# Two linear-attention and SwiGLU layers on one core: queries kept in matmul banks, and new order tables for the first layer

## The chip, the cores and the metric

The kernel runs on one core of one Trainium2 chip. The metric is the device time of one execution in microseconds. Five engines run their own queues of instructions and wait for each other by semaphores: PE (matrix products), DVE (elementwise and reductions), ACT (activations and scaled copies), POOL (elementwise) and SP, which here only issues DMAs. PE writes its products into eight banks of 128 x 512 fp32 numbers; all other tiles lie in one on-chip arena.

## What is computed

```python
def _A_ref(x, wqkv, wo):                       # H = 32 heads of 16, S = 2048, D = 512
    q, k, v = ...                              # x @ wqkv, by head
    phi = lambda t: jnp.where(t > 0, t + 1, jnp.exp(t)) + 1e-6
    pq, pk = phi(q), phi(k)
    kv = jnp.einsum("bhsd,bhse->bhde", pk, v)
    z = jnp.einsum("bhsd->bhd", pk)
    num = jnp.einsum("bhqd,bhde->bhqe", pq, kv)
    den = jnp.einsum("bhqd,bhd->bhq", pq, z)[..., None] + 1e-6
    return (num / den) @ wo                    # heads joined again
def _B_ref(x, w1, w3, w2):                     # F = 1792
    return (silu(x @ w1) * (x @ w3)) @ w2
x = x + _A_ref(_layernorm(x), ...)
x = x + _B_ref(_layernorm(x), ...)
x = x + _A_ref(_layernorm(x), ...)             # same weights again
x = x + _B_ref(_layernorm(x), ...)
```

## The kernel before

The 2048 rows are 16 tiles of 128 rows. Every product is made of three fp16 products (high x high, low x high, high x low), so each operand is first split: a high part (an fp16 copy, by ACT or POOL) and a low part (value minus high part, a subtraction with two rows as inputs, by DVE or POOL).

One layer has four stages. The **key stage** normalises a tile, splits and transposes it, projects it, forms phi(k) and adds it into a gram matrix. The **state stage** turns the gram matrix into one 512 x 512 matrix that holds keys, values and the output weights (`m_s`), and starts the first queries. The **query loop** does the rest of the 16 query tiles. The **MLP** works on four chunks of 512 rows with a seven-product scheme for blocks of two by two; its row sums (`mlp_rows`) and its products for group after group follow, and layer 0 also prepares the MLP's weights meanwhile.

In the profile of before, layer 0's key stage is 0 to 112 us, its queries 112 to about 230, its MLP until about 600; layer 1's queries are 714 to about 810.

A query tile t goes through these steps (L numbers are lines of before):

- `query(t)`: PE projects it into a bank `pq` (12 matmuls); ACT writes exp (L848, name `e`) and Relu (L849, name `r`) of the bank into two rows of the arena; SP loads the tile for t + 3.
- `phi_q(t)`: DVE joins them, min(e, 1) + r (L864).
- `weigh_in(t)`: DVE multiplies by the key sums z (L1175) and sums each head into `den` (L1178).
- `weigh_out(t)`: reciprocal (L1191), product with it (L1192, on DVE or POOL by the table `norm`), high part (L411 on ACT or L413 on POOL), low part (L1197 on POOL), and a DMA that transposes both (L1202).
- `attn_out(t)`: PE's 12 matmuls with `m_s` into a bank `po`; `attn_add(t)`: DVE adds it to x (L1212), ACT forms mean and squares (L1216, L1217).

Two pools of four banks exist: "w" (`bank`), which serves `pk`, `pq`, `po` of the attention and `ba`, `bb`, `bc` of the MLP in turn, and "acc" (`acc_bank`), which serves the gram sums, the products `pm`, and the MLP's output sums.

The order in the attention is written out and pinned on all five engines: `STATE` and `KEYS` name the steps, and `LOOP` the steps of one turn of the query loop. In layer 0 that is

```python
LOOP = ("p i v f f q o w f a", ...)   # p phi_q(t+3), i weigh_in(t+3), q query(t+4), o attn_out(t),
                                      # w weigh_out(t+3), a attn_add(t), f fill, v settle
```

Each `f` takes the next entry of `FILLS` and does that many pieces of other work: "1" and "2" are steps of the weight preparation (scales, splits L421 and L423, sums L549 to L555 of the weights' blocks, bounds), "r" a step of the first chunk's MLP rows (L1240 to L1243 sums, L1247 high and L1253 low parts). A weight scale is a reduction over partial maxima on DVE (L357), a small product on PE that spreads it (L360, `pm_w`), and small DVE steps (L362 and on). `ENGINES` gives the engine of each numbered step. In the MLP a planner orders the instructions; `HOOKS` gives how much weight work and how many row steps go behind each group, and how late they are due; `TURN` is the order of a group's products P1 to P7 and the copies (L1311) and sums (L1314) out of their banks.

## Time and profile before

| | us |
|---|---|
| runs | 1210.6, 1213.26, 1214.08 (median 1213.26) |
| profiled execution | 1208.15 |
| its span, first to last instruction | 1206.4 |
| PE busy in it | 1147.9 (95%) |
| DVE, ACT, POOL busy | 857.2, 634.8, 474.3 |
| mean granted PE clock | 0.996 |

Busy time is an average over stages with different limits. PE is idle in few places, and only there can another engine set the time; so the table is to be read with views by stretch and by wait. A name such as `arena` is the one on-chip tile that holds nearly all rows, so lines tell more than names do.

### The profile page before, as it was taken

To read this page: it belongs to the slowest core of one execution; us is meant where nothing else is said; L and a number is where in the kernel's file an instruction comes from. 1 tells how busy PE (TensorE), PEld (TensorE's weight loads), DVE (VectorE), ACT (ScalarE), POOL (GpSimd) and SP (SyncE) were. 2 spreads that over 40 slices of the span, in tenths; PEclk is the share of its full clock that TensorE was granted. 3 is DMA by queue.
4 is the path that set the end of the run, shared out by engine and by line. 5 is a ranking of instruction groups with operands and counts; after the bars stand their busy time and mean duration, and the time that the engine had idled before them with its cause. 6 is when DMAs were issued, how large, how long until landed. Compare 5 with 4: busy or idle time off the path is not lost.

```text
span 1206.4 us, 21781 instructions
## 1 busy us (share of the span) xinstructions
PE 1147.9 (95%) x8852; PEld 863.4 (72%) x8852; DVE 857.2 (71%) x1363; ACT 634.8 (53%) x1066; POOL 474.3 (39%) x520
## 2 busy tenths in 40 slices
PE   5999988889999989999999999989899999999998
PEld 2444533678888878888874454447788888888887
DVE  5787999867788897667775459966766745757443
ACT  5677576846454454433456644576543444444432
POOL 5351689721102113233558823885632122012010
PEclk9999998999999999999999999999999999999999
DMA  8976456669732222211306433564432340211000
GB/s 258 331 213 227 114 146 108 156 205 340 225 118 83 95 78 72 113 62 62 80 6 205 105 110 87 110 153 123 128 75 95 151 157 28 80 63 52 1 36 36
DMA packets 163396, 147.43 MB, mean 122 GB/s; under 512 B 129632, under 2 KB 138976, under 8 KB 158688
## 3 DMA queue, kind: packets, MB, share of 16 engines
q1 hardware_dynamic: 163296, 146.04, 41.3%
q8 instruction: 69, 1.13, 0.4%
q14 instruction: 31, 0.25, 0.1%
HBM read 72.48 MB, written 42.07 MB: 95 GB/s over the span
## 4 chain that ended last, share of the span: by engine, by line
PE 61%; DVE 19%; ACT 7%; POOL 6%; DMA 3%; issue 3%; SPq 0%; POOLq 0%; DVEq 0%; ACTq 0%
PE bb L499 19%; PE po L1358 15%; PE bc L499 10%; PE ba L499 5%; PE pk L499 4%; PE gt L499 4%; PE po L1378 3%; DMA arena<-arena 2%; DVE arena L423 2%; DVE arena L1175 2%; POOL arena L1197 1%; DVE arena L864 1%; DMA arena<-in_B_w_dram 1%; DVE den L1178 1%; ACT arena L421 1%
## 5 line engine op out<-in xcount | busy, mean ns | idle before, releaser
L499 PEld LDWEIGHTS <-arena 128*128 128x128 f16 x6360 | 619.7, 98 | 276.6 <-issue 32.6
L499 PE MATMUL bb<-arena 128*128 128x256 f16 x2688 | 332.6, 273 | 8.2 <-ACT arena L1311 6.5
L1358 PE MATMUL po<-arena 128*128 128x256 f16 x1932 | 236.7, 273 | 10.1 <-ACT arena L1270 8.6
L1358 PEld LDWEIGHTS <-arena 128*128 128x128 f16 x1932 | 188.0, 98 | 35.5 <-ACT arena L1270 10.6
L1311 ACT ACTIVATE arena<-bb 128x512 f32<-128x512 f32 x196 | 115.0, 589 | 164.6 <-PE bb L499 134.4
L1272 DVE TENSOR_TENSOR arena<-arena 128x512 f16<-128x512 f32 (+1 forms) x108 | 124.5, 1154 | 98.9 <-ACT arena L1270 98.6
L499 PE MATMUL bc<-arena 128*128 128x256 f16 x1344 | 165.7, 273 | 5.7 <-DVE arena L1212 3.7
L1270 ACT ACTIVATE arena<-arena 128x512 f16<-128x512 f32 x112 | 99.6, 890 | 91.1 <-DVE arena L1285 38.1
L1427 POOL TENSOR_TENSOR arena<-arena 128x512 f32<-128x512 f32 x29 | 44.3, 1528 | 255.3 <-DVE arena L1407 233.7
L1266 ACT ACTIVATE arena<-arena,scalars 128x512 f32<-128x512 f32 x112 | 74.7, 667 | 103.1 <-DVE arena L1314 102.7
L1267 DVE SCALAR_TENSOR_TENSOR arena<-arena,scalars 128x512 f32<-128x512 f32 x112 | 84.8, 757 | 50.6 <-ACT arena L1266 50.3
L1314 DVE TENSOR_TENSOR arena<-arena,bc 128x512 f32<-128x512 f32 x112 | 76.4, 682 | 51.7 <-ACT arena L1311 45.2
L1407 DVE SCALAR_TENSOR_TENSOR arena<-po,scalars,arena 128x256 f32<-128x256 f32 (+1 forms) x170 | 91.6, 585 | 13.4 <-PE po L1358 10.9
L499 PE MATMUL po<-arena 128*128 128x512 f16 x384 | 89.8, 384 | 6.3 <-DMA arena<-arena 4.7
L499 PE MATMUL pk<-arena 128*128 128x512 f16 x384 | 90.0, 386 | 3.2 <-DMA arena<-arena 1.9
L499 PE MATMUL pq<-arena 128*128 128x512 f16 x384 | 89.1, 384 | 0.7 <-DMA arena<-xt_d 0.7
L499 PE MATMUL gt<-arena 128*128 128x512 f16 x384 | 87.8, 379 | 1.6 <-ACT arena L920 1.0
L499 PE MATMUL ba<-arena 128*128 128x256 f16 x672 | 86.4, 273 | 0.0
L476 ACT ACTIVATE arena<-arena,nb_all,rs_all 128x512 f32<-128x512 f32 x64 | 50.4, 807 | 33.7 <-POOL nb_all L473 30.7
L423 DVE SCALAR_TENSOR_TENSOR arena<-arena,scalars 128x512 f16<-128x512 f32 (+2 forms) x60 | 53.2, 901 | 20.5 <-ACT arena L421 20.4
L1253 POOL TENSOR_TENSOR arena<-arena 128x512 f16<-128x512 f32 (+2 forms) x30 | 46.5, 1574 | 36.6 <-DMA arena<-arena 36.1
L1378 PE MATMUL po<-arena 128*128 128x256 f16 x480 | 57.0, 273 | 1.3 <-DVE arena L1272 1.0
(152 smaller groups left out, 1295.9 us busy)
## 6 DMA issues: line engine op xcount, KB each, us to landing
arena<-xb_d SPq DMA_DIRECT2D x12, 1792.0 KB, 6.8
xb_d<-arena SPq DMA_DIRECT2D x8, 1792.0 KB, 6.2
xt_d<-arena SPq DMA_DIRECT2D x32, 256.0 KB, 2.4
arena<-xt_d SPq DMA_DIRECT2D x32, 256.0 KB, 2.9
arena<-in_B_w_dram SPq DMA_DIRECT2D x8, 896.0 KB, 6.4
arena<-in_B_w_dram SPq DMA_DIRECT2D x28, 256.0 KB, 3.2
w_d<-arena SPq DMA_DIRECT2D x4, 1792.0 KB, 10.0
arena<-w_d SPq DMA_DIRECT2D x4, 1792.0 KB, 6.7
```

The lines of the kernel that those rows point to most:

```text
L423: lambda: nc.vector.scalar_tensor_tensor(lo, src, scale, hi, OP.mult, OP.subtract)
L476: nc.scalar.activation(dst, x_sb[:, t, :], AF.Identity, scale=rs_all[:, t : t + 1], bias=nb_all[:, t : t + 1],)
L499: nc.tensor.matmul(dst, lhs(a, k), rhs(b, k), start=first and k == 0 and i == 0, stop=last and k == n - 1 and i == len(PASSES) - 1, skip_g ...
L1266: nc.scalar.activation(t, gate, AF.Silu, scale=info["u1"])
L1267: nc.vector.scalar_tensor_tensor(t, up, info["hid"], t, OP.mult, OP.mult)
L1270: nc.scalar.activation(hs[:, 0, lo:hi], t[:, lo:hi], AF.Copy)
L1272: engine.tensor_tensor(hs[:, 1, lo:hi], t[:, lo:hi], hs[:, 0, lo:hi], OP.subtract)
L1311: nc.scalar.activation(dst, bank_, AF.Copy)
L1314: nc.vector.tensor_tensor(dst, dst, bank_, OP.add)
L1358: nc.tensor.matmul(po[:, i * HALF : (i + 1) * HALF], hs[:, a, qx, cs], w2[:, b, qw, :], start=g == ends[0] and i + a + b == 0, stop=g == e ...
L1378: nc.tensor.matmul(acc[n][:, half * HALF : (half + 1) * HALF], hs[:, a, qx, cs], w2_a21[g][:, b] if (i, half) == (0, 1) else w2[:, b, i + ...
L1407: nc.vector.scalar_tensor_tensor(dst, src, cb, to, OP.mult, OP.add)
```

## The change

For tiles from 4 on (`DEEP`), `query` takes its bank from the "acc" pool and the tile's rows stay in it: ACT's Relu overwrites the bank, DVE's join reads e from the arena and r from the bank and writes the bank, and `weigh_in` multiplies there (if the tile is normalised on POOL it writes the arena row instead). The product with the reciprocal reads the bank and writes the arena row of e. Both layers do this. A variant of phi for POOL (`phi_plain`, its scalar `nuq` and its table) is dropped; no tile used it.

```diff
-    def phi_act(ps, u, eps):
-        e, r = f32("kept"), f32()
+    DEEP = 4
+    def phi_act(ps, u, eps, in_bank=False):
+        e, r = f32("kept"), ps if in_bank else f32()
...
-    def phi_sum(e, r, eps):
+    def phi_sum(e, r, eps, to=None):
+        to = e if to is None else to
...
-            nc.vector.scalar_tensor_tensor(e, e, 1.0, r, OP.min, OP.add)
+            nc.vector.scalar_tensor_tensor(to, e, 1.0, r, OP.min, OP.add)
...
     def query(t):
-        pp = bank("pq")
+        pp = acc_bank("pq") if t >= DEEP else bank("pq")
...
+        pqs[t] = phi_act(pp, info["uq"], False, t >= DEEP)
...
     def phi_q(t):
+        e, r = pqs[t]
+        if t >= DEEP:
+            phi_sum(e, r, False, r)
+        else:
+            pqs[t] = phi_sum(e, r, False), None
     def weigh_in(t):
-        pq = pqs[t]
-        nc.vector.scalar_tensor_tensor(pq, pq, EPS, zb, OP.add, OP.mult)
+        e, pp = pqs[t]
+        pq = e if pp is None or engine_of("norm", t) is nc.gpsimd else pp
+        nc.vector.scalar_tensor_tensor(pq, e if pp is None else pp, EPS, zb, OP.add, OP.mult)
...
     def weigh_out(t):
+        low = engine_of("natlow", t)
+        to = e if low is nc.gpsimd else pq
         engine_of("norm", t).tensor_tensor(
-            pq_h, pq_h, den[:, :, None].to_broadcast([P, H, DH]), OP.mult
+            by_head(to), by_head(pq), den[:, :, None].to_broadcast([P, H, DH]), OP.mult
         )
```

Layer 0's tables `STATE`, `ENGINES`, `KEYS`, `FILLS`, `TURN` and `HOOKS` are written anew; layer 1 keeps its own. In `ENGINES` the row sums of chunks 1 and 2 go from POOL to DVE, three high parts of keys go from POOL to ACT, and some steps change places.

```diff
-            "f s r h t f n l"
+            "f s r t h f n l"
...
-            "sums:VVVVVVVVVVVVVVVVVVPPPPPVPVVP rowsum:PPPPPPPP rowlow:PPVVVVVV "
+            "sums:VVVVVVVVVVVVVVVVVVPPPPPVPVVP rowsum:PPVVVVPP rowlow:PPVVVVVV "
...
-            "P1 a P2 P6 P5 c P7 b b+ m a+ P4 P3 s c+ C D n o h e"
+            "P1 a P6 P2 P5 c P7 b b+ m P4 a+ P3 s c+ n C D o h e"
```

DVE in layer 0's query loop, the turn with tile 11 in it, before: join, product with z, head sums, then the reduction for the scale of w2 (`pt_w_104`), reciprocal, product, and the add of tile 8.

```order
L864 SCALAR_TENSOR_TENSOR arena<-arena 128x512
L1175 SCALAR_TENSOR_TENSOR arena<-arena 128x512
L1178 TENSOR_REDUCE den<-arena 128x32
L357 TENSOR_REDUCE scalars<-pt_w_104 128x1
L1191 RECIPROCAL den<-den 128x32
L1192 TENSOR_TENSOR arena<-arena,den 128x512
L1212 SCALAR_TENSOR_TENSOR arena,total<-po,scalars,arena 128x512
```

DVE now, the next turn (tile 12), where that reduction now stands (L859, L1167, L1169, L1188 and L1211 are the lines L864, L1175, L1178, L1192 and L1212 of before; L423 are weight splits).

```order
L859 SCALAR_TENSOR_TENSOR pq<-arena,pq 128x512
L1167 SCALAR_TENSOR_TENSOR pq<-pq,arena 128x512
L1169 TENSOR_REDUCE den<-pq 128x32
L423 SCALAR_TENSOR_TENSOR arena<-arena,scalars 128x2x256
L357 TENSOR_REDUCE scalars<-pt_w_104 128x1
L1184 TENSOR_SCALAR den<-den 128x32
L1185 RECIPROCAL den<-den 128x32
L1188 TENSOR_TENSOR arena<-pq,den 128x512
L423 SCALAR_TENSOR_TENSOR arena<-arena,scalars 128x2x128
L1211 SCALAR_TENSOR_TENSOR arena,total<-po,scalars,arena 128x512
```

The reduction moved by one turn, from tile 11's to tile 12's. On PE its product `pm_w` stood ahead of the query of tile 13 and now stands ahead of that of tile 15, two turns later.

DVE at the end of the loop, between the adds of tiles 11 and 12, before:

```order
L1212 SCALAR_TENSOR_TENSOR arena,total<-po,scalars,arena 128x512
L864 SCALAR_TENSOR_TENSOR arena<-arena 128x512
L1175 SCALAR_TENSOR_TENSOR arena<-arena 128x512
L1178 TENSOR_REDUCE den<-arena 128x32
L1191 RECIPROCAL den<-den 128x32
L1253 TENSOR_TENSOR arena<-arena 128x512
L1253 TENSOR_TENSOR arena<-arena 128x256
L1192 TENSOR_TENSOR arena<-arena,den 128x512
```

The same place now (L1239 to L1242 are the row sums L1240 to L1243 of before, L1252 is L1253); only the first twelve of the twenty rows up to tile 12's add are shown.

```order
L1211 SCALAR_TENSOR_TENSOR arena,total<-po,scalars,arena 128x512
L859 SCALAR_TENSOR_TENSOR pq<-arena,pq 128x512
L1239 TENSOR_TENSOR arena<-arena 128x256
L1241 TENSOR_TENSOR arena<-arena 128x256
L1167 SCALAR_TENSOR_TENSOR pq<-pq,arena 128x512
L1240 TENSOR_TENSOR arena<-arena 128x256
L1169 TENSOR_REDUCE den<-pq 128x32
L1242 TENSOR_TENSOR arena<-arena 128x256
L1252 TENSOR_TENSOR arena<-arena 128x512
L1252 TENSOR_TENSOR arena<-arena 128x256
L1185 RECIPROCAL den<-den 128x32
L1252 TENSOR_TENSOR arena<-arena 128x1024
```

Row sums of the MLP's second chunk, which stood in POOL's queue, stand between the steps of tile 15, and the chunk's third low part ahead of its normalisation; three more sums follow before tile 12's add. In all 16 row sums left POOL for DVE.

## The prediction

> **What bounds the kernel now.** I read the page's first part, then the stretches, then who waits for whom, then single instructions. The first part says which engine can set the time.

> ```profile
> PE 1147.9 (95%) x8852; PEld 863.4 (72%) x8852; DVE 857.2 (71%) x1363; ACT 634.8 (53%) x1066; POOL 474.3 (39%) x520
> ```

> PE is idle for 58.5 us of 1206.4; the change adds and removes no matmul, so only these, and the time that PE runs slowly, can be won or lost. Next the stretches (length; busy PE, PEld, DVE, ACT, POOL; granted clock; DMA share; GB/s): layer 0's queries, their end, the turn into the MLP, then the same of layer 1.

> ```profile
> 139.00:175.00 36.00, 36.00 (x169) 16.33 (x167) 32.78 (x57) 27.05 (x63) 27.27 (x25) 1.00 0.59 153
> 175.00:215.00 40.00, 30.51 (x142) 14.42 (x141) 38.41 (x55) 25.31 (x52) 36.98 (x30) 0.91 0.59 105
> 215.00:250.00 35.00, 26.82 (x209) 20.51 (x209) 29.80 (x39) 27.61 (x51) 24.70 (x27) 0.98 0.73 212
> ...
> 739.00:786.00 47.00, 47.00 (x219) 21.31 (x218) 43.41 (x75) 25.50 (x55) 35.54 (x37) 1.00 0.57 117
> 786.00:805.00 19.00, 15.22 (x87) 8.01 (x85) 16.23 (x25) 11.96 (x27) 16.77 (x17) 1.00 0.57 113
> ```

> PE never pauses from 139 to 175, so a faster DVE buys nothing there. From 175 to 250 it is idle for 17.7 us, with DVE at 96% and POOL at 92% in the first 40 us. Layer 1 is the same on a smaller scale: no pause until 786, then 3.8 us. The waits, first of 170 to 260, then of PE alone in 786 to 900 (total, times, longest, us):

> ```profile
> PE pm_w L360 <- DVE scalars L357: 3.8, 1, 3.8
> ...
> ACT arena L1247 <- POOL arena L1243: 3.8, 1, 3.8
> ...
> PE po L499 <- DMA arena<-arena: 3.5, 2, 3.2
> ...
> PE bb L499 <- ACT arena L1311: 3.3, 1, 3.3
> ...
> PE bc L499 <- DVE arena L1212: 1.8, 1, 1.8
> ...
> PE po L499 <- DVE arena L1212: 1.6, 1, 1.6
> ...
> PE bb L499 <- DMA arena<-arena: 1.5, 1, 1.5
> ...
> PE po L1358 <- ACT arena L1270: 3.3, 2, 2.4
> PE bc L499 <- DVE arena L1212: 1.9, 1, 1.9
> ...
> PE po L499 <- DMA arena<-arena: 1.2, 2, 0.6
> PE pq L499 <- DMA arena<-xt_d: 0.7, 1, 0.7
> ```

> The idle gaps also cost clock. Each of the three waits over 3 us in layer 0 is followed by slices below 1.00 (the column before the last two):

> ```profile
> 180.00:185.00 5.00, 4.62 (x15) 1.98 (x16) 4.57 (x9) 4.78 (x10) 4.83 (x5) 0.66 0.96 152
> ...
> 200.00:205.00 5.00, 3.77 (x11) 1.39 (x12) 4.83 (x6) 3.40 (x8) 5.00 (x4) 0.66 1.17 149
> ...
> 245.00:250.00 5.00, 1.69 (x12) 1.18 (x10) 3.15 (x4) 3.65 (x6) 2.02 (x4) 0.89 1.00 422
> ```

> A third of 5 us is 1.7 us lost per dip (the last dip runs on past 250; I take it as long). The stretch thus holds 17.7 + 5.1 = 22.8 us.

> **Why DVE and POOL are slow there.** Durations (min/median/max ns, then groups with busy us, mean ns): whole kernel, then 139 to 223, then 739 to 803.

> ```profile
> L864 DVE SCALAR_TENSOR_TENSOR arena<-arena x32: 679/710/2350, 118.8 to 795.4; 128x512 f32<-128x512 f32 x32
> ...
> L1314 DVE TENSOR_TENSOR arena<-arena,bc x112: 649/683/690, 226.0 to 1191.0; 128x512 f32<-128x512 f32 x112
> ...
> L1178 DVE TENSOR_REDUCE den<-arena x32: 686/686/687, 120.6 to 799.3; 128x32 f32<-128x512 f32 x32
> ...
> L1197 POOL TENSOR_TENSOR arena<-arena x32: 1151/1480/1605, 124.2 to 806.1; 128x512 f16<-128x512 f32 x32
> ...
> L423 DVE SCALAR_TENSOR_TENSOR arena<-arena,scalars 128x512 f16<-128x512 f32 x14 | 14.8, 1070 | 1.8 <-ACT arena L421 1.7
> L1175 DVE SCALAR_TENSOR_TENSOR arena<-arena 128x512 f32<-128x512 f32 x12 | 14.1, 1176 | 0.4
> L864 DVE SCALAR_TENSOR_TENSOR arena<-arena 128x512 f32<-128x512 f32 x12 | 12.4, 1036 | 1.0 <-ACT arena L849 0.9
> ...
> L1192 DVE TENSOR_TENSOR arena<-arena,den 128x512 f32<-128x512 f32 x6 | 6.2, 1041 | 0.1
> ...
> L1175 DVE SCALAR_TENSOR_TENSOR arena<-arena 128x512 f32<-128x512 f32 x12 | 14.6, 1215 | 0.4
> L864 DVE SCALAR_TENSOR_TENSOR arena<-arena 128x512 f32<-128x512 f32 x12 | 11.7, 973 | 2.3 <-ACT arena L849 1.9 <-ACT nm_all L1216 0.4
> ...
> L1192 DVE TENSOR_TENSOR arena<-arena,den 128x512 f32<-128x512 f32 x8 | 6.3, 794 | 0.3
> ```

> DVE instructions with two full rows in SBUF (L864, L1175, L1192, L423) spread from 0.68 to 2.35 us. Those with one row in a bank (L1314, 112 of them) or with one row in all (L1178) never stray from 0.65 to 0.69, whatever POOL does. POOL's own two-row step L1197 varies likewise, 1.15 to 1.60. The pairing of two SBUF rows on DVE with two on POOL is what costs; the change takes one row of three such DVE steps into a bank.

> **The change, part by part.**

> Layer 0's DVE. Tiles 4 to 15: 12 + 12 + 6 = 30 instructions, 14.1 + 12.4 + 6.2 = 32.7 us; at L1314's 0.68 they take 20.4, so 12.3 us less. What PE gets is read at three gates.

> Gate 1, PE's out product of tile 12 (the 3.2 us wait for a transpose at 198). Ahead of it stands POOL's chain to tile 12's low half:

> ```profile
> 176.00:198.00 22.00, 18.23 (x77) 7.81 (x75) 21.23 (x35) 15.03 (x31) 21.74 (x18) 0.92 0.48 91
> ...
> 196.30 1.60 POOL L1197 TENSOR_TENSOR arena<-arena 128x512 f16<-128x512 f32 x1
> ...
> L499 PE MATMUL pq<-arena 128*128 128x512 f16 x384 | 89.1, 384 | 0.7 <-DMA arena<-xt_d 0.7
> ```

> POOL is busy for 21.74 of 22 us, at 1.60 for a step that can take 1.15: at most 28%, 6.1 us, is contention. Of DVE's two-row work in 139 to 223, 32.7 us of 47.5 (with L423) leaves, so 69% of 6.1 = 4.2 us. The moved w2 scale product (pm_w) frees 3.8 + 1.7 us ahead of this gate: its reduction is issued one tile later and its matmul two, so it gains one tile of slack, and a tile is two products of 12 matmuls at 89.1 / 384 = 0.232 us, 5.6 us, over 3.8. But PE then only arrives earlier at the gate. Gain here 4.2, between 0 and 6.1.

> Gate 2, the first bc bank at 214 to 216, freed by DVE's residual add of tile 12 (L1212). DVE from the add of tile 7 to that of tile 11:

> ```profile
> 175.55 0.75 DVE L1212 SCALAR_TENSOR_TENSOR arena<-po,scalars,arena 128x512 f32<-128x512 f32 x1
> ...
> 207.59 0.74 DVE L1212 SCALAR_TENSOR_TENSOR arena<-po,scalars,arena 128x512 f32<-128x512 f32 x1
> ```

> 32.0 us. The new order holds for the same four tiles 16 full rows at 0.69 (L1178's), six and a half weight rows and four adds at 0.75 (L1212's), and reciprocals and small rows, by my estimate a quarter of a full row for each of 16: 11.0 + 7.9 + 2.8 = 21.7, so 10.3 earlier at best; the weight rows stay contended, say 8. Then seven 256-wide row sums and one more low part (1024 wide) stand ahead of tile 12's add: 7 x 0.42 + 2 x 0.69 = 4.3 (0.42 is L780, the smallest mean of that shape; the last fence). Net 4 to 6 earlier. Gates 1 and 2 agree on about 5: taken 5, from 1 to 8.

> Gate 3, 216 to 250: waits of 1.6 (L1212 of tile 13: two weight rows and a row sum stand between it and tile 12's add, where a low part and three longer steps stood: gone) and 3.3 + 1.7 of clock. In the latter ACT sits 3.8 us on POOL's fourth row sum with the bank copy L1311 queued behind it. First and last of those four sums:

> ```profile
> 240.00 1.64 POOL L1240 TENSOR_TENSOR arena<-arena 128x256 f32<-128x256 f32 x1 [1.23 <-DVE arena L1253]
> ...
> 244.51 1.05 POOL L1243 TENSOR_TENSOR arena<-arena 128x256 f32<-128x256 f32 x1
> ```

> They took 5.6 us; on DVE 4 x 0.42 = 1.7 if nothing is ahead of them. DVE is 85% busy there, so half: 2.5. Sum 4.1, from 0 to 8.

> Layer 1 has only the bank rows, its tables stay. 32 instructions, 14.6 + 11.7 + 6.3 = 32.6 us, less 32 x 0.68 = 21.8: 10.8 us off a DVE that lags PE by under 4. Waits of 0.7 + 1.2 + 1.9 = 3.8 at 786 to 802 go except the load of xt_d, which stands in SP's queue behind transposes: gain 3, from 0 to 3.8. The 3.3 behind L1270 follow from the MLP's own order: 0.

> What could cost. (a) ACT's Relu and DVE's sum and product now write a bank; no row shows either engine doing so. I bound it by 0.1 less and 0.1 more each (twice L1314's spread), for DVE's two +-2.4 us per layer; taken 0, since the bank reads nearest to it (L1314) cost nothing. (b) PE's query product now waits for the bank of the query four tiles before, that is for DVE's product or normalisation, in place of ACT's Relu of two before. At the 3.8 us wait PE stood at query 13 and DVE at the weighing of tile 11, one tile late; four banks cover that: 0; without the cover one tile, 5.6. (c) The po products have the other four banks to themselves: included in gates 2 and 3. (d) The exponential still writes one of two rows that POOL's low part frees: unchanged. (e) P6 ahead of P2 in a group puts ACT's copy of bb directly between two products into bb, a copy's time in each of 28 groups were nothing between. PE's built order in the middle of the MLP is nearly what it was, with out products in between: 0, up to +2. (f) Key stage, engine swaps, SP's order: same work, +-1.5.

> ```profile
> L780 DVE TENSOR_TENSOR arena<-arena 128x256 f32<-128x256 f32 x8 | 3.4, 420 | 0.0
> ...
> L1284 DVE TENSOR_TENSOR arena<-arena 128x256 f32<-128x256 f32 x1 | 0.9, 941 | 0.0
> ```

> Sum: 5 + 4.1 + 3 = 12.1 us. The profiled execution took 1208.15 us (span 1206.4 and 1.75 around it), so 1196; the median of the three runs shown, 1213.26, lies 5.1 above it, and against that 1201.

> [...]

> **The rivals.** 0.3%, 3.6 us, is about what a measurement of this kernel can tell from no change.

> A. DVE is relieved, but the row sums and POOL's remaining work set gates 1 to 3, so only part comes through: gate 1's 4 and layer 1's 2. For it: POOL at 99% up to gate 1, and its list of work there is nearly the same. Against: that work is itself contended. 1207.

> B. Nothing to see: the three freed steps leave L423 and POOL's steps to collide as often, each wait ends on the next late thing (transposes, xt_d loads). For it: five kinds of wait stand within 50 us of each other. Against: L1178 and L1314, 144 instructions without a stretched one. 1213.

> C. Slower. Sixteen row sums with two SBUF rows now stand in DVE's queue at the turn, two low parts of them ahead of tile 15's normalisation, and wait for ACT's high parts. At L1284's contended 0.94 they cost 15 us; it decides once they exceed the 10 us that DVE has gained by 208, and the excess of 5, with 1.7 of clock, less layer 1's 3, gives 1217. For it: L1284. Against: POOL loses these sums, so it has less to collide with.

> D. All 22.8 us of the turn but 3 go, and layer 1's: some 1191. For it: pm_w's dip and all three clock dips hang on gaps barely over 3 us. Against: DVE's list up to tile 12's add is only 4 to 6 us shorter.

> **How the numbers follow.** Forecast (1197 to 1206) 0.55, A 0.20, B 0.12, C 0.06, D 0.07. Faster: 0.55 + 0.07 + nine tenths of A = 0.80. Same: the rest of A and nearly all of B, 0.13. Slower: C and a little of B, 0.07. The range leaves out B, C and the edge of D, 0.2: 1193 to 1210. The likeliest time is 1201.

> **What would show it.** Right: L864, L1175 and L1192's successors on tiles 4 to 15 within 0.65 to 0.80 us, with their maxima gone; no wait of PE for L357; L1197 nearer 1.2 than 1.48; PE idle of 175 to 250 at 8 to 11 instead of 17.7; one dip of the clock or none; at 786 to 802 under 1 us. Wrong: bank writes over 0.8 us; the new query product waiting for DVE; row sums on DVE at 0.9; PE's idle time the same with other names on it.

## The result, and the profile after

The changed kernel takes 1194.26 us (median of 4 runs, 1190.15 to 1196.56) against 1211.93 us (1210.03 to 1214.08) on the same chip: ratio 0.985, 95% interval 0.9816 to 0.9884, so 17.7 us less. The profiled pair differs by less: 1194.72 (span 1193.0) against 1208.15 (span 1206.4), 13.4 us.

In the changed kernel most line numbers are a little lower: the join L864 is L859, the product L1175 is L1167, the normalisation L1192 is L1188, POOL's low part L1197 is L1196, the residual add L1212 is L1211, the copy of bb L1311 is L1310; the row sums are L1239 to L1242, their low part L1252; the MLP's high part of a hidden tile is L1269 and the products behind it L1357 and L1377.

The page's first part:

```profile
PE 1147.0 (96%) x8852; PEld 865.6 (73%) x8852; DVE 841.3 (71%) x1380; ACT 636.8 (53%) x1068; POOL 432.0 (36%) x500
```

PE's busy time is as before; its idle time fell from 58.5 to 46.0 us, 12.5 of the 13.4. The same stretches as before (length; busy PE, PEld, DVE, ACT, POOL; granted clock; DMA share; GB/s):

```profile
139.00:175.00 36.00, 36.00 (x169) 16.28 (x168) 30.79 (x60) 29.36 (x67) 26.93 (x30) 1.00 0.68 161
175.00:215.00 40.00, 33.42 (x176) 17.81 (x175) 37.18 (x68) 29.73 (x61) 27.69 (x26) 0.96 0.70 153
215.00:250.00 35.00, 31.67 (x277) 27.43 (x275) 26.76 (x47) 24.26 (x43) 9.08 (x12) 0.95 0.70 206
739.00:786.00 47.00, 47.00 (x228) 22.14 (x227) 35.69 (x72) 29.07 (x61) 36.63 (x44) 1.00 0.63 126
786.00:805.00 19.00, 19.00 (x153) 14.73 (x152) 7.57 (x12) 16.09 (x31) 13.68 (x17) 1.00 0.69 182
```

From 175 to 250 PE's idle time is 9.9 us where it was 17.7. The changed kernel is 4 to 12 us ahead there, so the same stretch holds later work; between the same two points of the work, the first query product and the 101st matmul into a bank `bb` of the MLP, PE is idle for 10.7 us where it was 17.7. From 739 to 805, layer 1's queries and turn, PE never stops. DVE is busy for 7.7 us less in the first 47, but a part of this too is other work: at the same place of the work (the changed kernel begins layer 1's queries 12.9 us earlier, so 726 to 773) it is busy for 39.10 us, 4.3 less than before. Who waits, 170 to 260 and then PE alone from 786 to 900 (total, times, longest, us):

```profile
PE po L1377 <- ACT arena L1269: 3.3, 1, 3.3
PE bb L499 <- DMA arena<-arena: 3.3, 1, 3.3
PE po L499 <- DMA arena<-arena: 2.8, 2, 2.1
...
DVE arena L1252 <- DMA arena<-arena: 2.2, 1, 2.2
...
PE po L499 <- DVE arena L1211: 0.5, 1, 0.5
...
PE po L1357 <- ACT arena L1269: 3.5, 3, 2.7
PE bb L499 <- ACT arena L1310: 2.8, 3, 1.3
PE po L1357 <- DVE arena L1271: 1.3, 2, 0.8
PE bc L499 <- DVE arena L1313: 1.2, 1, 1.2
```

The wait for pm_w is gone, and so are layer 1's four waits at the turn. Two waits stand in new places: PE for the transposed row parts at 198 (3.31 us) and for the first hidden tile's high part at 226 (3.33 us). In layer 1's MLP PE waits more than before: 8.8 us from 805 to 900, where the same view had 6.2. Durations (ns, min/median/max):

```profile
L859 DVE SCALAR_TENSOR_TENSOR pq<-arena,pq x24: 690/691/697, 135.4 to 779.7; 128x512 f32<-128x512 f32 x24
...
L1167 DVE SCALAR_TENSOR_TENSOR pq<-pq,arena x14: 685/699/700, 165.6 to 770.5; 128x512 f32<-128x512 f32 x14
...
L1188 DVE TENSOR_TENSOR arena<-pq,den x14: 674/692/692, 168.2 to 772.6; 128x512 f32<-128x512 f32 x14
...
L1196 POOL TENSOR_TENSOR arena<-arena x32: 1152/1157/1606, 120.2 to 788.1; 128x512 f16<-128x512 f32 x32
...
L851 ACT ACTIVATE pq<-pq,scalars x24: 635/652/652, 130.4 to 777.1; 128x512 f32<-128x512 f32 x24
L851 ACT ACTIVATE arena<-pq,scalars x8: 676/680/689, 113.8 to 714.3; 128x512 f32<-128x512 f32 x8
```

The durations of a step with a row in a bank lie within 18 ns, POOL's low part has a median of 1157 where it had 1480, and a write to a bank costs DVE 8 ns (median 699 for L1167 into the bank, 691 for its executions that read the bank and write the arena) and saves ACT 28 ns (652 against 680).

### The profile page after: what moved, and what is told of

It is laid out like the page before. It is cut to its first block, busy times and chain, and to the rows that moved or that the text cites. A ratio compares the mean times of both kernels' runs of the same rounds, so it can differ in the third digit from the quotient of the medians.

```text
span 1193.0 us, 21773 instructions
## 1 busy us (share of the span) xinstructions
PE 1147.0 (96%) x8852; PEld 865.6 (73%) x8852; DVE 841.3 (71%) x1380; ACT 636.8 (53%) x1068; POOL 432.0 (36%) x500
## 4 chain that ended last, share of the span: by engine, by line
PE 70%; DVE 14%; ACT 6%; POOL 4%; DMA 4%; issue 2%; SPq 0%; DVEq 0%; POOLq 0%; ACTq 0%
PE bb L499 19%; PE po L1357 14%; PE bc L499 9%; PE pq L499 6%; PE po L499 5%; PE gt L499 5%; PE ba L499 4%; PE pk L499 4%; PE po L1377 3%; DMA arena<-arena 3%; DVE arena L1266 2%; DVE arena L1271 1%; DVE arena L1406 1%; DVE arena L1313 1%; ACT arena L1269 1%
## 5 line engine op out<-in xcount | busy, mean ns | idle before, releaser
L499 PEld LDWEIGHTS <-arena 128*128 128x128 f16 x6360 | 620.6, 98 | 262.9 <-issue 19.6
L499 PE MATMUL bb<-arena 128*128 128x256 f16 x2688 | 333.2, 274 | 6.5 <-DMA arena<-arena 3.3
L1357 PE MATMUL po<-arena 128*128 128x256 f16 x1932 | 237.3, 273 | 10.5 <-ACT arena L1269 8.2
L1357 PEld LDWEIGHTS <-arena 128*128 128x128 f16 x1932 | 188.4, 98 | 36.3 <-ACT arena L1269 10.4
L1310 ACT ACTIVATE arena<-bb 128x512 f32<-128x512 f32 x196 | 115.2, 590 | 165.5 <-PE bb L499 136.9
L499 PE MATMUL bc<-arena 128*128 128x256 f16 x1344 | 166.9, 274 | 1.9 <-DVE arena L1313 1.2
L1269 ACT ACTIVATE arena<-arena 128x512 f16<-128x512 f32 (+1 forms) x112 | 99.7, 891 | 98.1 <-DVE arena L1266 41.4
L1426 POOL TENSOR_TENSOR arena<-arena 128x512 f32<-128x512 f32 x28 | 40.3, 1441 | 285.5 <-DVE arena L1406 263.9
L1266 DVE SCALAR_TENSOR_TENSOR arena<-arena,scalars 128x512 f32<-128x512 f32 x112 | 87.5, 781 | 52.6 <-ACT arena L1265 52.5
L1313 DVE TENSOR_TENSOR arena<-arena,bc 128x512 f32<-128x512 f32 x112 | 76.4, 682 | 50.4 <-ACT arena L1310 45.8
L1406 DVE SCALAR_TENSOR_TENSOR arena<-po,scalars,arena 128x256 f32<-128x256 f32 (+1 forms) x170 | 91.7, 584 | 14.0 <-PE po L1357 11.4
L499 PE MATMUL pk<-arena 128*128 128x512 f16 x384 | 90.2, 387 | 2.8 <-DMA arena<-arena 2.2
L499 PE MATMUL po<-arena 128*128 128x512 f16 x384 | 87.8, 379 | 3.3 <-DMA arena<-arena 2.8
L499 PE MATMUL gt<-arena 128*128 128x512 f16 x384 | 87.8, 379 | 1.6 <-ACT arena L915 1.0
L499 PE MATMUL pq<-arena 128*128 128x512 f16 x384 | 87.4, 379 | 0.9 <-DVE arena L1044 0.9
L499 PE MATMUL ba<-arena 128*128 128x256 f16 x672 | 86.9, 274 | 0.0
L1377 PE MATMUL po<-arena 128*128 128x256 f16 x480 | 58.7, 277 | 3.3 <-ACT arena L1269 3.3
L423 DVE SCALAR_TENSOR_TENSOR arena<-arena,scalars 128x512 f16<-128x512 f32 (+2 forms) x60 | 50.3, 853 | 12.5 <-ACT arena L421 11.3
L1252 POOL TENSOR_TENSOR arena<-arena 128x512 f16<-128x512 f32 (+2 forms) x30 | 43.7, 1481 | 41.4 <-DMA arena<-arena 39.9
```

Of the source, the lines that this page charges most:

```text
L423: lambda: nc.vector.scalar_tensor_tensor(lo, src, scale, hi, OP.mult, OP.subtract)
L499: nc.tensor.matmul(dst, lhs(a, k), rhs(b, k), start=first and k == 0 and i == 0, stop=last and k == n - 1 and i == len(PASSES) - 1, skip_g ...
L1266: nc.vector.scalar_tensor_tensor(t, up, info["hid"], t, OP.mult, OP.mult)
L1269: nc.scalar.activation(hs[:, 0, lo:hi], t[:, lo:hi], AF.Copy)
L1310: nc.scalar.activation(dst, bank_, AF.Copy)
L1313: nc.vector.tensor_tensor(dst, dst, bank_, OP.add)
```

## Experiments

Each kernel was timed against the kernel before, whose median in these comparisons lay between 1210.6 and 1211.4 us; the ratio is given with its 95% interval. The changed kernel's own interval is wide (0.9816 to 0.9884), so a difference from it of 2 us settles nothing. Every profile is of one execution. The first four kernels take the change apart.

**e1_bank_part**: the code as changed, layer 0's six tables as before.

```diff
-"... nat:PPAPAPPPAPPAAAAA key:PPPPPPAAPAAAAPPA ... rowsum:PPVVVVPP ..."
+"... nat:PPAAPPPAAPPAAAAA key:PPPPPPAAPPPAPPPA ... rowsum:PPPPPPPP ..."
... STATE, KEYS, FILLS, TURN, HOOKS of layer 0 likewise
```

> The changed kernel with layer 0's tables of before: the bank part alone. Theory 1 (the rows in banks end DVE's and POOL's stretched steps, and that carries most of the gain): 8 to 12 us faster than before, POOL's low part near 1.16 us, the wait for pm_w down from 3.8 us to under 1, since DVE reaches its scalars' step 4 to 6 us earlier; layer 1 gives its 3.8 in any case. Theory 2 (the newly chosen tables carry layer 0's gain): 4 us faster, layer 1's share alone, with layer 0's three waits over 3 us and three clock dips still there. Theory 3 (queries' own banks, not where the rows lie): as theory 1 in time; run e4 tells them apart.

Measured: 1198.91 us, ratio 0.9906 (0.9891 to 0.9921), 11.4 us faster (9.6 to 13.2). PE's waits from 170 to 260:

```profile
PE bb L499 <- ACT arena L1310: 3.3, 1, 3.3
PE po L499 <- DMA arena<-arena: 2.4, 1, 2.4
PE bb L499 <- DMA arena<-arena: 2.0, 1, 2.0
PE po L1377 <- DVE arena L1271: 1.0, 1, 1.0
PE bc L499 <- DVE arena L1266: 0.7, 1, 0.7
```

The wait for pm_w is gone with the scale product at its old place, and so are the two waits for the residual add. The wait for the bb copy behind POOL's row sums is unchanged. POOL's low part has a median of 1157 ns. This is theory 1's time, and theory 3's as well; e4 tells these two apart.

**e2_tables_part**: the code before, layer 0's tables as changed.

```diff
-"... rowsum:PPPPPPPP ..."
+"... rowsum:PPVVVVPP ..."
... STATE, KEYS, FILLS, TURN, HOOKS of layer 0 likewise
```

> The kernel before with layer 0's new tables: the tables alone. Theory 1: 3 to 6 us faster (the pm_w wait of 3.8 us with its clock dip goes, and four row sums leave POOL, but DVE's steps stay stretched to 1.0 to 1.2 us in the mean), layer 1 unchanged with 3.8 us of pauses at its turn. Theory 2: 12 to 14 us faster. A third outcome, 0 or slower: the new tables fit only a DVE that the bank rows have relieved, and the row sums on DVE come late.

Measured: 1205.05 us, ratio 0.996 (0.9946 to 0.9974), 4.8 us faster, within theory 1's 3 to 6. But not for its reason: in the profile PE still waits 3.5 us for pm_w, though the product stands two queries later, 3.8 for a residual add and 4.2 for the bb copy, and its idle time from 175 to 250 is 17.2 us, against 17.7 before. PE's three longest waits from 170 to 260:

```profile
PE bb L499 <- ACT arena L1311: 4.2, 1, 4.2
PE po L499 <- DVE arena L1212: 3.8, 1, 3.8
PE pm_w L360 <- DVE arena L1212: 3.5, 1, 3.5
```

**e3_bank_layer1**: the tables of before, bank rows in layer 1 only.

```diff
-    DEEP = 4
+    DEEP = (NT, 4)
...
-        pp = acc_bank("pq") if t >= DEEP else bank("pq")
+        pp = acc_bank("pq") if t >= DEEP[state["layer"]] else bank("pq")
```

> The kernel before with bank rows in layer 1 only, every table as before. Theory 1: layer 1's four kinds of pause at its turn (3.8 us) go and nothing takes their place: 3.5 to 4 us faster. Rival: the later MLP waits take part of it back (in the changed kernel a wait of 2.7 us stood where 2.4 and 0.9 had stood, with a clock dip of 1.7 us after it): 1.5 to 2.5 us faster.

Measured: 1205.78 us, ratio 0.9962 (0.9949 to 0.9975), 4.6 us faster (3.0 to 6.2). PE never stops from 739 to 805. The dip of the clock that the rival puts behind the wait of 2.7 us stands elsewhere in the changed kernel, at 857, behind two waits of 1.30 and 1.18 us; in this run no dip comes between 437 and 1200.

The three can be compared at points that all kernels pass, among them the first query product and the wait of 2.94 us in layer 0's MLP. Rows of before, the changed kernel, e1 and e2 for the first two points (start, duration, engine, line):

```profile
112.38 1.89 PE L499 MATMUL pq<-arena 128*128 128x512 f16 x8
...
434.31 1.59 PE L1358 MATMUL po<-arena 128*128 128x256 f16 x13 [2.95 <-ACT arena L1270]
```

```profile
108.77 2.54 PE L499 MATMUL pq<-arena 128*128 128x512 f16 x11
...
419.58 2.45 PE L1357 MATMUL po<-arena 128*128 128x256 f16 x13 [2.94 <-ACT arena L1269]
```

```profile
112.58 2.75 PE L499 MATMUL pq<-arena 128*128 128x512 f16 x12
...
426.09 1.97 PE L1357 MATMUL po<-arena 128*128 128x256 f16 x13 [2.94 <-ACT arena L1269]
```

```profile
109.38 1.89 PE L499 MATMUL pq<-arena 128*128 128x512 f16 x8
...
428.49 1.59 PE L1358 MATMUL po<-arena 128*128 128x256 f16 x13 [2.94 <-ACT arena L1270]
```

With a third point between them (the 101st matmul into bb, counted in the traces) and three later ones, the lead over before in us is

| point | before at | e1, banks | e2, tables | e1 + e2 | changed | e3 |
|---|---|---|---|---|---|---|
| first query product | 112.4 | -0.2 | 3.0 | 2.8 | 3.6 | 0.0 |
| 101st matmul into bb | 249.8 | 8.7 | 2.2 | 10.9 | 12.3 | 0.2 |
| wait of 2.94 in the MLP | 434.3 | 8.2 | 5.8 | 14.0 | 14.7 | 0.8 |
| layer 1's first query product | 711.6 | 7.1 | 5.1 | 12.2 | 12.9 | -0.1 |
| layer 1's MLP, after its first wait over 2 us | 827.5 | 11.0 | 4.6 | 15.6 | 16.9 | 3.9 |
| end of the span | 1206.4 | 9.9 | 3.9 | 13.8 | 13.4 | 2.7 |

The two parts add, as far as single executions can show: e3 runs the program of before up to layer 1 and still differs by up to 0.8 us there. The bank rows are worth 8.7 us at layer 0's turn and 4 at layer 1's: from its first query product to the point in its MLP PE takes 112.0 us in all eleven kernels with bank rows there, and 115.9 to 116.5 in the three without (before, e2, e4). The tables are worth 3.0 to 3.6 in the key stage and nothing at the turn. Between 250 and 434 they bring another 2.4 to 3.6, but by layer 1's first query only 0.6 of this is left in the changed kernel, and 2.9 in e2: behind the wait of 2.94 us the changed kernel pays a dip of the clock that before and e2 do not have (last section). After layer 1's turn each of the four gives back 0.7 to 3.5 us.

**e4_rows_sbuf**: the changed kernel, with its tables and its assignment of banks, but Relu row, sum and product in the arena.

```diff
-        pqs[t] = phi_act(pp, info["uq"], False, t >= DEEP)
+        pqs[t] = phi_act(pp, info["uq"], False)
...
-        if t >= DEEP:
-            phi_sum(e, r, False, r)
-        else:
-            pqs[t] = phi_sum(e, r, False), None
+        pqs[t] = phi_sum(e, r, False), None
```

> The changed kernel with its tables and its assignment of banks (queries from tile 4 on in the accumulator banks), but the Relu row, the sum and the product written to SBUF rows as before. Theory 1 (contention of SBUF rows): DVE's three steps and POOL's low part are stretched again (means 1.0 to 1.2 and 1.4 to 1.5 us in the queries' last third), layer 1's pauses come back in part, 8 to 14 us slower than the changed kernel, so 4 to 9 us faster than before. Theory 3 (the banks' assignment carries the gain, since out products have four banks to themselves and a query product waits for nothing late): within 3 us of the changed kernel, 15 to 18 us faster than before.

Measured: 1205.91 us, ratio 0.9964 (0.9953 to 0.9975): 12 to 14 us slower than the changed kernel, and as fast as e2. From the first query product to the 101st matmul into bb it takes 138.4 us, before 137.4, the changed kernel 128.8. Its product, join and POOL's low part (ns):

```profile
L1164 DVE SCALAR_TENSOR_TENSOR arena<-arena x32: 677/1042/2515, 115.3 to 793.6; 128x512 f32<-128x512 f32 x32
...
L859 DVE SCALAR_TENSOR_TENSOR arena<-arena x32: 679/783/2345, 114.2 to 791.3; 128x512 f32<-128x512 f32 x32
...
L1193 POOL TENSOR_TENSOR arena<-arena x32: 1147/1480/1607, 119.8 to 801.9; 128x512 f16<-128x512 f32 x32
```

So it is where the rows lie that counts, not who owns the banks: the same steps in the same order are stretched again, DVE's up to 2.5 us and POOL's to a median of 1.48. That POOL's work is what stretches DVE's can be read from the same traces. Of e4's products, joins and normalisations by DVE with both rows in the arena, the 24 during which POOL did nothing took 0.68 to 0.69 us, and the 35 with POOL busy beside them for over nine tenths of their time 0.69 to 2.52. In the changed kernel 33 such steps with one row in a bank ran with POOL busy beside them for as long, and took 0.68 to 0.70. The profile of before splits like e4's: 19 such steps with POOL idle took 0.68 to 0.69 us, and 38 with POOL busy for over nine tenths of their time 0.69 to 2.35. The product has a median of 1042 ns in e4, against 699 in the changed kernel with its row in a bank.

The next four undo one part of the tables each within the changed kernel.

**e5_sums_pool**: layer 0's row sums all on POOL.

```diff
-rowsum:PPVVVVPP
+rowsum:PPPPPPPP
```

> The changed kernel with all of layer 0's row sums on POOL again (in the changed kernel the third to sixth pair of row halves is summed on DVE). The changed kernel's ratio to before is 0.985. Theory 1 (gate 3 as forecast: POOL's row sums hold up ACT and, behind it, the copy of bb): 2 to 4 us slower than the changed kernel, ratio 0.987 to 0.988, with PE waiting again some 3 us for the bb copy. Rival (the third rival's mechanism in small: four row sums on DVE took 1.46, 1.49, 1.15 and 0.77 us in the changed kernel, where 0.41 is the least, just ahead of PE's wait of 3.3 us for bb at 198): equal or up to 3 us faster than the changed kernel, ratio 0.982 to 0.985.

Measured: 1198.47 us, ratio 0.9892 (0.9877 to 0.9907), some 4 to 5 us slower than the changed kernel. The size is theory 1's, the place is not. At the turn POOL's sums are the better ones: the 101st matmul into bb starts at 235.2 us against 237.5, and PE waits 1.9 us for the transposed rows where it waited 3.3. The loss comes later, in the same MLP. PE's waits from 340 to 625, first of this kernel, then of the changed one:

```profile
PE po L1357 <- ACT arena L1269: 4.5, 2, 3.8
PE bc L499 <- DVE arena L1313: 3.8, 3, 2.1
...
```

```profile
PE po L1357 <- ACT arena L1269: 3.8, 4, 2.9
PE po L1357 <- DVE arena L1406: 0.7, 1, 0.7
...
```

The planner orders the whole MLP of layer 0 anew when sums move (DVE's order differs there), and in the new one PE waits 8.5 us in this stretch, 3.7 more. The longest of these waits runs into a half-clock stretch of 6.83 us at 609 (granted clock 0.94 from 600 to 660), which costs up to 3.4 us more. That the planner's order would be worse for any such move is not shown.

**e6_fills_old**: layer 0's `FILLS` as before (the w2 scale product ahead of query 13).

```diff
-"... - - - - 2 12 2r 1 - 2 112 r2 - - - 22 - rr - 1 r2 - 1 1 r2 ..."
+"... - - - - 1 22 - r2 - 12 1 r122 - - - 22 - rr - 21 r2 1 1 - r ..."
```

> The changed kernel with layer 0's filler table of before: the w2 scale product (pm_w) stands ahead of query 13 again, and the other fillers where they stood. Theory 1 (the bank rows have brought DVE forward, and no wait for pm_w is left to remove, as in the run with the bank part alone): within 1.5 us of the changed kernel, ratio 0.984 to 0.986, no wait of PE for L357 over 1 us. Rival (the later place is what removes the wait): 4 to 6 us slower than the changed kernel, ratio 0.988 to 0.990, with a wait of 3 us or more for L357 and a clock dip.

Measured: 1197.61 us, ratio 0.9887 (0.9872 to 0.9902): the rival's time, without its mechanism. No wait for L357 is left after 135. The first query product starts at 111.62 us, 2.9 later than in the changed kernel; PE's waits from 60 to 135:

```profile
PE pz L874 <- DVE arena L929: 1.0, 1, 1.0
PE pq L499 <- DVE arena L1044: 0.8, 1, 0.8
PE pm_w L360 <- DVE scalars L357: 0.7, 1, 0.7
PE pk L499 <- DVE scalars L362: 0.7, 1, 0.7
PE pk L499 <- ACT arena L847: 0.4, 2, 0.2
```

The pm_w of this list is an earlier scale at 98 us. `FILLS` also places the weight preparation within the key stage, and there undoing it costs 2.9 us.

**e7_turn_old**: layer 0's `TURN` as before.

```diff
-"P1 a P6 P2 P5 c P7 b b+ m P4 a+ P3 s c+ n C D o h e"
+"P1 a P2 P6 P5 c P7 b b+ m a+ P4 P3 s c+ C D n o h e"
```

> The changed kernel with layer 0's order of steps in a group of the MLP as before (P2 ahead of P6, and the rest of that row). Theory A (read from the traces: PE's waits of 1.6 and 2.0 us at 325 and 334 stand in every kernel with the old table and are 0.9 in all in those with the new): 2 to 3 us slower than the changed kernel, ratio 0.9865 to 0.9875. Theory B (the forecast's term: the copy of bb stands directly between two products into bb): 0 to 2 us faster than the changed kernel, ratio 0.983 to 0.985.

Measured: 1192.56 us, ratio 0.9849 (0.9829 to 0.9869), no difference from the changed kernel. PE's waits between 250 and 345 are 1.3 us in all (1.8 in the changed kernel, 3.6 before). So the new order of a group costs nothing that can be told, and is not what removed the waits of 325 and 334 either.

**e9_keys_old**: layer 0's `STATE` and `KEYS` as before.

```diff
-            "f s r t h f n l"
+            "f s r h t f n l"
... and STATE of layer 0
```

> The changed kernel with the two tables of layer 0's key stage and of its hand-over to the queries as before (STATE and KEYS). Theory A (read from the traces: PE's waits of 0.9, 1.5 and 0.7 us between 67 and 99 stand in every kernel with the old tables, and 0.6 and 0.8 in those with the new): 1.5 to 2.5 us slower than the changed kernel, ratio 0.986 to 0.987. Theory B (the forecast's term: the same work, plus or minus 1.5, and whatever PE gains at 99 it waits for at the turn): within 1 us of the changed kernel.

Measured: 1195.45 us, ratio 0.9869 (0.9853 to 0.9886). By the ratios this is 2.3 us slower than the changed kernel, theory A's size, by the medians 1.2, and the intervals overlap. The profile has the place: the first query product is back at 112.36 us, 3.6 later, and a wait of 2.5 us for the bb copy stands at 314. But the profiled execution, 1199.88 us, is the slowest of the four (the others 1194.91 to 1195.7), and has a dip of the clock at 23 us (granted clock 0.99 from 0 to 139) that costs up to 1.7 of the 3.6. e5 and e10, with the new `STATE` and `KEYS`, have such a dip at 22 us too, and start their queries at 109.4 and 109.2.

Undone one at a time, the row sums, `FILLS`, and `STATE` with `KEYS` lose 4.2, 3.4 and 1.2 us by the medians; e1, with every table undone, loses 4.7. So their gains do not add: the tables fit each other, and undoing one can cost nearly as much as undoing all. `HOOKS` and the other changes of `ENGINES` were not undone alone.

The last four try to take away the two new waits.

**e10_low3_pool**: the fourth low part of the MLP's rows (chunk 1, second half) on POOL.

```diff
-rowlow:PPVVVVVV
+rowlow:PPVPVVVV
```

> The changed kernel with the fourth low part of layer 0's MLP rows on POOL instead of DVE. In the changed kernel DVE's queue stands 2.2 us at this low part (L1252 at 224.9, waiting for the transpose that still reads its buffer) and then works 2.4 us on it, with the gate-up product L1266 and the high part L1269 behind it, and PE waits 3.33 us at 226 for that high part, with a clock dip of 1.7 us. Theory 1 (this wait in DVE's queue is what took the place of gate 3's wait): PE's wait at 226 falls under 1.5 us and its dip goes, 3 to 5 us faster than the changed kernel, ratio to before 0.981 to 0.983. Rival (the first group's own chain of products, copies and high part is as long as that, whoever makes the low part; in the run with the row sums on POOL the wait was still 2.4): within 1.5 us of the changed kernel, ratio 0.984 to 0.987.

Measured: 1197.35 us, ratio 0.988 (0.9865 to 0.9895), 3 to 4 us slower. PE's wait at 226 is still 2.8 us, so DVE's queue behind that low part was not what set it, or not alone. The rival's reason holds for the wait; its time misses too, because new waits came at 284 to 303. PE's longest from 170 to 340:

```profile
PE po L1377 <- ACT arena L1269: 4.1, 3, 2.8
PE bb L499 <- ACT arena L1310: 3.9, 3, 2.4
PE bb L499 <- DMA arena<-arena: 2.6, 2, 1.6
PE po L499 <- DMA arena<-arena: 2.1, 1, 2.1
...
```

**e11_low1_dve**: the second low part (chunk 0, second half) on DVE.

```diff
-rowlow:PPVVVVVV
+rowlow:PVVVVVVV
```

> The changed kernel with the second low part of layer 0's MLP rows on DVE instead of POOL. In the changed kernel POOL makes it from 191.4 to 195.3 behind query 13's low part, its transpose is issued at 195.6, and PE waits 3.31 us at 198 for it. Theory 1 (POOL's queue sets this wait): the transpose starts 2 to 3 us earlier, PE's wait at 198 falls to about 1 us with its clock dip gone, 2 to 4 us faster than the changed kernel, ratio 0.982 to 0.983. Rival (DVE was 93% busy from 175 to 215, two SBUF rows of this low part run into POOL's weight sums and cost 1 us or more each, and the residual add of the query before comes later): equal or up to 4 us slower, ratio 0.985 to 0.988.

Measured: 1192.97 us, ratio 0.9842 (0.9827 to 0.9856), not to be told from the changed kernel. The wait at 198 fell from 3.31 to 0.50 us as theory 1 has it. What followed is the rival's time: PE then waited 1.7 us for the bb copy at 201, 0.9 for L1313, and 1.9 at 319. Its waits from 170 to 340 sum to 11.7 us, in the changed kernel also to 11.7.

**e12_low1_low3**: both moves.

```diff
-rowlow:PPVVVVVV
+rowlow:PVVPVVVV
```

> Both moves together: the second low part of layer 0's MLP rows on DVE and the fourth on POOL. If theory 1 holds for both, the gains add: 5 to 8 us faster than the changed kernel, ratio 0.978 to 0.981. If a wait removed at 198 only brings PE earlier to the wait at 226, the better of the two alone.

Measured: 1197.62 us, ratio 0.9882 (0.9865 to 0.9898): the worse of the two alone, against both expectations. PE's waits of 170 to 340 sum to 15.8 us.

**e13_low1_turn**: e11's move with e7's order.

```diff
-rowlow:PPVVVVVV
+rowlow:PVVVVVVV
...
-"P1 a P6 P2 P5 c P7 b b+ m P4 a+ P3 s c+ n C D o h e"
+"P1 a P2 P6 P5 c P7 b b+ m a+ P4 P3 s c+ C D n o h e"
```

> The changed kernel with the second low part of layer 0's MLP rows on DVE and the old order of steps in a group of layer 0's MLP. Alone they gave 0.9842 and 0.9849, against the changed kernel's 0.985. Theory 1 (what is left at the turn and in layer 0's MLP are separate small waits, and the new order of steps only happened to fit the new tables): the two add to some 2 to 3 us, ratio 0.982 to 0.983, with PE's waits at 319 (1.9 us) and at 226 under 1.5 us. Rival (the waits there are one chain, and each edit only moves the idle time of some 10 us between 175 and 330): 0.984 to 0.986, PE's idle time of 175 to 330 within 1.5 us of that of the kernel with the one edit.

Measured: 1193.89 us, ratio 0.9865 (0.9848 to 0.9881): the rival. PE's waits of 170 to 340 are 11.8 us. No kernel tried is faster than the changed one by more than the measurement can tell.

## Why the prediction was right, and where its sum was not

The forecast was 12.1 us in the profiled pair; 13.4 came. Against the median it was 12.3 us (1213.26 to 1201), and 17.7 came, 1194.26 us, inside the range of 1193 to 1210 but faster than the 1197 to 1206 that was held likeliest. The mechanism stands: bank rows end the stretched steps (e4), and that is worth 11.4 us by itself (e1). But some terms hit for the wrong reason, and that the sum came so close in the profiled pair is partly luck. By the table it was 3.6 (key stage) + 8.7 (gates) + 0.6 (layer 0's MLP) + 4.0 (layer 1) - 3.5 (the MLP after it) = 13.4, where the forecast had 0 + 9.1 + 0 + 3 + 0; the first and the last, both priced at nothing, cancel.

- **DVE's steps at 0.68, POOL's low part nearer 1.2.** Right: medians of 0.69 to 0.70 and 1.16.
- **Gates 1 to 3, 9.1 us.** Right in size only. The bank rows alone gave 8.7 us by 250. Gates 1 and 2 were sized at 5 of these, and 2.5 of gate 3's 4.1 were put down to the row sums on DVE. e5 and e2 show that the sums bring nothing there (2.3 us the other way in e5): in the changed kernel four sums of chunk 1 took 1.46, 1.49, 1.15 and 0.77 us at 195 to 201. That is rival C's collision, in its place, on four of its sixteen sums; the eleven of the sixteen beside which POOL did nothing took 0.41 to 0.42, and so did one beside which POOL worked. The gates' gain is the banks', 8.7 where 5 + 1.6 had been theirs.
- **pm_w's move frees nothing at the turn.** Right, and more so: e1 shows the wait gone without the move, and e2 the wait still there with it.
- **Layer 1, 3 us (0 to 3.8).** A little too small: 4.6 (3.0 to 6.2) in e3, 4.0 in the profiles; the wait for the load of xt_d, which was expected to stay, went too.
- **The MLP after it, 0.** Wrong: the changed kernel leads by 16.9 us in layer 1's MLP after its first long wait and by 13.4 at the end. PE's matmuls stand there in the same order as before, and wait some 2.5 us longer; a dip of the clock at 857 comes on top. e3, with only layer 1's rows changed, gives back 1.2 us of 3.9. From that point to the end before takes 378.9 us and e2 379.6, the eleven kernels with bank rows in layer 1 take 380.0 to 382.4, and e4, whose rows lie in the arena but whose queries have the other banks, 381.6. So an earlier PE is not needed for the loss; whether the order of banks makes it was not tried, and the cause stays open.
- **(a) bank writes, 0 +-2.4.** Right, nearly 0: 8 ns more for a write by DVE, 28 less for one by ACT.
- **(b) the query product's wait for a bank, 0.** A wait of 0.78 us at 126 (behind L1044, which frees a `pm` bank) came, once; none later.
- **(e) TURN, 0 to +2.** Right: e7 cannot be told from 0.
- **(f) key stage and swaps, +-1.5.** The step that failed. The tables are worth 3.6 us at the first query product. With the old fillers (e6) 2.9 of it are lost, with the old `STATE` and `KEYS` (e9) as much as 3.6, a dip of the clock included, so they win it only together. The forecast had priced "same work" instead of reading PE's waits of 0.9, 1.5 and 0.7 us at 67 to 99 as time that an order could win. Between 250 and layer 1's first query the tables bring 0.6 (changed) to 2.9 us (e2) more. Which of them does so stays open: with `TURN` old it is there, and in e9's profile it is lost.
- **One dip of the clock or none.** Wrong: there are two at the turn, at 202 and 229, two later, at 420 and 857, and one that starts 1.4 us before the end, where before had three, all at the turn. The last section has the reason.

## What to carry to other kernels

Where DVE's steps read two on-chip rows and POOL works beside them (in the kernel before 0.69 to 2.35 us a step, with POOL idle 0.68 to 0.69), leave one operand of DVE's step in the bank in which its product already lies. Both engines gained here (medians of 699 ns for the product where e4 has 1042, and 1157 for POOL's low part where it has 1480), but the kernel gains only at the places where the matrix engine waits for them. Before pricing a new order at zero, add up the matrix engine's small waits in that stage: they are what an order can win. Tables that were chosen together are judged together: undone one at a time, they do not show each one's worth. At a turn where several chains end within some microseconds of each other, a wait taken away singly is waited for elsewhere (11.7 us before and after in e11), so such an edit has to be timed, not added up.

## What the runs showed of the hardware

```profile
429.78:433.19 3.41, 1.58 (x15) 1.17 (x12) 2.53 (x5) 2.29 (x3) 0.00 (x0) 1.00 0.00 0
433.19:436.60 3.41, 2.29 (x21) 2.07 (x22) 3.41 (x5) 2.05 (x3) 0.00 (x0) 1.00 0.49 154
```

```profile
416.74:420.15 3.41, 0.57 (x6) 0.52 (x7) 2.79 (x3) 3.26 (x4) 0.00 (x0) 1.00 0.15 25
420.15:423.56 3.41, 3.41 (x19) 2.43 (x17) 2.95 (x5) 1.84 (x3) 0.00 (x0) 0.50 0.35 129
...
853.64:857.05 3.41, 1.34 (x11) 0.90 (x10) 2.20 (x2) 1.66 (x2) 3.33 (x4) 1.00 0.13 38
857.05:860.46 3.41, 3.00 (x15) 2.07 (x15) 3.41 (x7) 1.71 (x3) 0.35 (x1) 0.50 0.02 5
```

Before, the wait falls across two cells (idle 1.83 and 1.12 us) and costs no clock; in the changed kernel it falls into one (2.84) and costs a dip. At 854 two gaps of 1.30 and 1.18 us put 2.07 us of idle time into one cell, and a dip follows. In these two profiles 468 cells begin between 100 and 900 us: the seven with 2.07 us or more of idle time were followed by a dip, and none of the others, which had up to 1.90 (before, at 798). Counted over the 14 profiles of this study there are 3278 cells between 100 and 900 us: all 48 with 2.05 us or more of idle time were followed by a dip, 4 of 18 with 1.85 to 2.05, and of those with less none of the 3157 at full clock; the other 55 lay within a dip, and three of them were followed by another. Part of the scatter of a kernel's runs may thus be the grid's phase, at an estimated 1.7 us or less a dip (half of 3.413 us, from the clock of 0.50); only one execution of each was profiled, so this was not shown.
